# Whole score blocks, two-DMA clears and later head rows in a fused retention and mixture-of-experts kernel

## The chip, the cores and the metric

The kernel runs on one core of a Trainium2 chip. The metric is the device time of one execution in microseconds; the time of a kernel is the median of its runs.

## The reference

```python
# retention: B=4, H=8 heads, S=768, D=64, per-head decay gamma
for t in range(S):
    state = gamma * state + outer(k[:, :, t], v[:, :, t])
    y[:, :, t] = scale * (q[:, :, t] @ state)
x = y.transpose(0, 2, 1, 3).reshape(3072, 512)
# experts: E=8, D=512, F=1024; each token goes to one expert
logits = x @ w_gate
e_idx  = argmax(logits)
gate_w = softmax(logits)[e_idx]
eom    = sigmoid(x @ w_output_gate)
for e in range(8):
    mask = e_idx == e
    out[mask] = gate_w[mask] * eom[mask, e] * (relu(x[mask] @ w1[e]) @ w2[e])
```

## The kernel before

**Retention loop.** The 768 positions of a sequence are cut into six chunks of 128; four sequences give 24 steps (`NCH`), in two interleaved chains of sequences (`chunk`). In each step `n` TensorE multiplies the carried state with the queries (`inter`), forms the scores of the chunk (`scores`), turns the next chunk's keys (`kt_block`), multiplies the masked scores with the scaled values (`values`) and adds to the state (`state`). VectorE masks the scores (`masked`) and scales the outputs (`outputs`); GpSimd (POOL) multiplies the values with decays (`prep_v`); ScalarE (ACT) evicts. The scores of a head pair are 128 keys by 128 queries. Keys are loaded in two halves, and for heads 4 to 7 the halves of the partitions are exchanged (`load_keys`, three DMAs a load). The scores are computed per half of the keys: one matmul over all 128 queries, one over the 64 queries that the causal mask leaves for the late half (`x == 1`).

**Routing.** Two steps make a group. Its gate logits are formed, turned, and each token gets an expert (`route1`), a place in that expert's region (`counts`, `route2`) and a gate (`exps`, `gates`). The finished row is scaled (`rows_out`) and sent by GpSimd to its place in a sorted buffer in DRAM, `srt` (`scatter`), some four steps behind. A stretch of each region (rows `FILL` to `TOP`) is cleared beforehand with zeros from `zrow` (`clear`); clears and scatters write the same tensor, so a scatter waits for the clears that stand before it in program order, and a clear for the scatters before it.

**Head.** At step 14 (`PICK_AT`) the expert with the most tokens so far is picked (`totals`, `rank`); its weights are loaded one block of the hidden dimension at a time (`load_weights`, three DMAs into a ring `raw`) and split into a high and a low part (`split_high` on ACT, `split_low` on VectorE and GpSimd). At step 20 its first 256 rows are read back (`head_load`) and turned on VectorE (`head_prep`). Behind the loop, the expert's matmuls on these rows (`run_head(n)` issues n of them) are written between the last groups' routing and the ranking of all experts; `counts` and `totals` of the last group come there too.

**Experts.** The eight experts follow in ranked order (`mm1`, `mm2`, `relu1`), the first with 192 rows, the others with up to 448. Weights are loaded ahead as far as the ring allows.

The order on every engine is the order of the program, written by hand (`manual_schedule`); loads are issued by SyncE (SP) in order, `load_k(n + 3)` and `load_v(n + 3)` at the head of step `n`. Rings: keys 6, values 4, scaled values 3, raw weights 3.

## Time and profile before

| | us |
|---|---|
| median of 3 runs (480.23 to 483.4) | 480.68 |
| the profiled execution's own time | 483.37 |
| its span, first to last instruction | 481.4 |
| TensorE busy | 425.5 (88%) |
| VectorE busy | 227.5 (47%) |
| ScalarE busy | 190.3 (40%) |
| GpSimd busy | 254.1 (53%) |
| SyncE's queue of loads, share of 16 DMA engines | 53.5% |

The span is one execution on the chip. Busy times overlap between engines; a matmul's end is modelled, so a busy TensorE need not be at its peak.

### The profile page before, as it was taken

How to read it: one execution, taken by the hardware profiler on the slowest of the kernel's cores; microseconds unless marked ns; L12 is line 12 of the kernel's file. 1: busy time of each engine (PE TensorE's matmuls, PEld its weight loads, DVE VectorE, ACT ScalarE, POOL GpSimd, SP SyncE). 2: the span in 40 equal slices, each digit the busy share in tenths (PEclk: the TensorE clock that was granted, in tenths of full speed). 3: DMA queues.
4: the chain of work that ended last, by engine and by line, in shares of the span. 5: the costliest groups of instructions: out<-in, count | busy, mean ns of one | idle time of the engine just before them, and what ended most of it. 6: DMA issues, size and time to landing. Idle time of an engine off the chain costs nothing.

```text
span 481.4 us, 11599 instructions
## 1 busy us (share of the span) xinstructions
PE 425.5 (88%) x4080; PEld 393.9 (82%) x4080; DVE 227.5 (47%) x586; ACT 190.3 (40%) x375; POOL 254.1 (53%) x290
## 2 busy tenths in 40 slices
PE   7799359989895877979999999999999999999892
PEld 3578348768784777969999999999999999999771
DVE  3255045657664664427545445445445356354020
ACT  2346116545664231136434344345344444353010
POOL 3430165443661760363642667667676775885602
PEclk9799779999999689979999999999999999999987
DMA  6798788889874423835874864855855956850101
GB/s 149 161 203 205 196 217 212 192 206 224 206 199 119 131 107 91 169 92 155 204 168 121 178 174 142 188 173 155 197 149 154 222 164 174 206 164 21 46 1 67
DMA packets 130594, 75.85 MB, mean 158 GB/s; under 512 B 59444, under 2 KB 118200, under 8 KB 130496
## 3 DMA queue, kind: packets, MB, share of 16 engines
q1 hardware_dynamic: 124624, 61.54, 53.5%
q0 software_dynamic: 5136, 12.64, 7.7%
q8 instruction: 65, 1.06, 1.0%
q10 hardware_dynamic: 736, 0.34, 0.3%
q14 instruction: 33, 0.27, 0.2%
HBM read 59.73 MB, written 15.30 MB: 156 GB/s over the span
## 4 chain that ended last, share of the span: by engine, by line
PE 65%; DMA 7%; issue 7%; SPq 7%; DVE 6%; POOL 3%; ACT 2%; another core or an unknown queue 2%; POOLq 0%; DVEq 0%; ACTq 0%
PE h L859 24%; PE a L882 23%; PE y L380 4%; DMA kn<-in_k_dram 3%; SPq L243 3%; PE s L587 2%; PE y L345 2%; PE y L569 2%; POOL out_dram L200 1%; SPq L241 1%; PE px L491 1%; DMA vn<-in_v_dram 1%; DMA srt<-zrow 1%; PE s L359 1%
## 5 line engine op out<-in xcount | busy, mean ns | idle before, releaser
L193 POOL TENSOR_TENSOR wlo<-raw,whi 128x512 fp32r<-128x512 f32 x64 | 84.9, 1328 | 67.7 <-ACT whi L185 58.9
L200 POOL DMA_INDIRECT out_dram<-ot,idi x85 | 85.0, 1000 | 20.2 <-issue 18.5
L859 PE MATMUL h<-xw,whi 128*128 128x192 f32 (+7 forms) x256 | 86.0, 336 | 0.9 <-issue 0.7
L859 PE MATMUL h<-xh,whi 128*128 128x192 f32 (+7 forms) x256 | 85.9, 336 | 0.9 <-PE s L587 0.9
L859 PE MATMUL h<-xh,wlo 128*128 128x192 f32 (+7 forms) x256 | 85.4, 334 | 0.0
L869 DVE SCALAR_TENSOR_TENSOR hl<-h,hh 128x192 fp32r<-128x192 f32 (+7 forms) x64 | 35.4, 554 | 96.9 <-ACT hh L868 81.8
L882 PE MATMUL a<-hh,whi 128*128 128x192 f32 (+6 forms) x224 | 75.1, 335 | 2.8 <-ACT hh L868 2.8
L882 PE MATMUL a<-hl,whi 128*128 128x192 f32 (+6 forms) x224 | 75.0, 335 | 0.0
L882 PE MATMUL a<-hh,wlo 128*128 128x192 f32 (+6 forms) x224 | 74.8, 334 | 0.0
L868 ACT ACTIVATE hh<-h 128x192 fp32r<-128x192 f32 (+7 forms) x64 | 31.1, 488 | 88.7 <-PE h L859 66.7
L507 POOL DMA_INDIRECT srt<-row,pos x24 | 25.0, 1041 | 68.8 <-DMA srt<-zrow 15.3
L192 DVE TENSOR_TENSOR wlo<-raw,whi 128x512 fp32r<-128x512 f32 x61 | 42.9, 704 | 31.5 <-ACT whi L184 15.0
L184 ACT CAST whi<-raw 128x512 fp32r<-128x512 f32 x64 | 39.5, 618 | 45.4 <-PE a L882 25.8
L859 PEld LDWEIGHTS h<-xh,whi 128*128 128x128 f32 x256 | 49.1, 192 | 1.9 <-PE s L587 1.1
L859 PEld LDWEIGHTS h<-xw,whi 128*128 128x128 f32 x256 | 49.0, 192 | 1.9 <-issue 0.8
L859 PEld LDWEIGHTS h<-xh,wlo 128*128 128x128 f32 x256 | 49.1, 192 | 0.2
L370 DVE TENSOR_TENSOR am<-s,mask 128x512 f32<-128x512 f32 x48 | 30.9, 684 | 35.0 <-PE s L362 32.7
L882 PEld LDWEIGHTS a<-hh,whi 128*128 128x128 f32 x224 | 42.9, 191 | 3.4 <-ACT hh L868 3.0
L882 PEld LDWEIGHTS a<-hh,wlo 128*128 128x128 f32 x224 | 42.8, 191 | 0.3
L882 PEld LDWEIGHTS a<-hl,whi 128*128 128x128 f32 x224 | 42.7, 191 | 0.4
L380 PE MATMUL y<-am,vs 128*64 128x128 f32 x384 | 30.4, 305 | 13.8 <-DVE am L370 6.8
L185 ACT CAST whi<-raw 128x512 fp32r<-128x512 f32 x64 | 39.5, 617 | 0.4 <-DMA raw<-in_moe_w_dram 0.3
(160 smaller groups left out, 674.0 us busy)
## 6 DMA issues: line engine op xcount, KB each, us to landing
raw<-in_moe_w_dram SPq DMA_DIRECT2D x128, 128.0 KB
raw<-in_moe_w_dram SPq DMA_DIRECT2D x64, 256.0 KB
qn<-in_q_dram SPq DMA_DIRECT2D x12, 512.0 KB
kn<-in_k_dram SPq DMA_DIRECT2D x24, 128.0 KB
kn<-in_k_dram SPq DMA_DIRECT2D x48, 64.0 KB
vn<-in_v_dram SPq DMA_DIRECT2D x24, 128.0 KB
vn<-in_v_dram SPq DMA_DIRECT2D x48, 64.0 KB
xl<-srt SPq DMA_DIRECT2D x12, 209.6 KB
```

The lines of the kernel that those rows point to most:

```text
L184: nc.scalar.copy(hi[:, 0], raw[:, 0])
L185: nc.scalar.copy(perm(hi), r2)
L192: (first or nc.vector).tensor_sub(lo[:, 0], raw[:, 0], hi[:, 0].bitcast(F32))
L193: nc.gpsimd.tensor_sub(perm(lo), r2, perm(hi).bitcast(F32))
L200: st = nc.gpsimd.indirect_dma_start(out=dst, out_offset=bass.IndirectOffsetOnAxis(ap=idx, axis=0), in_=src, in_offset=None, bounds_check=n ...
L370: nc.vector.tensor_tensor(out=a.rearrange("p s o t -> p s (o t)"), in0=sp[b].rearrange("p (s x) -> p s x", s=2), in1=mask.rearrange("p o t ...
L380: nc.tensor.matmul(py(o, b, S_), vs[n][:, 2 * g + b], a[b][:, S_, o], start=(c == 0 and S_ == 0), stop=True, skip_group_check=True)
L507: s_ = nc.gpsimd.indirect_dma_start(out=srt, out_offset=bass.IndirectOffsetOnAxis(ap=rt.pop(("pos", i)), axis=0), in_=row.rearrange("p a x ...
L859: nc.tensor.matmul(ps[:, 0:C], l[:, 0, w], r[:, dc, 0:C], start=(n == 0), stop=(n == 3 * NDC - 1))
L868: nc.scalar.activation(hh, ps[:, 0:C], AF.Relu)
L869: nc.vector.scalar_tensor_tensor(out=hl, in0=ps[:, 0:C], scalar=0.0, in1=hh.bitcast(F32), op0=ALU.max, op1=ALU.subtract)
L882: nc.tensor.matmul(accs[d][:, 0:C], l[:, 1, w], r[:, 0:C], start=(f == 0 and n == 0), stop=(f == NF - 1 and n == 2))
```

## The change

- Keys and values are loaded whole, one DMA for each load, without the exchange of halves; the first values go through ACT's DMA queue, as does the clearing. The value decays are loaded straight into place.
- The scores of a head are one block of 128 keys by 128 queries: eight matmuls a step with 64 rows of contraction and 128 columns of weights, in place of sixteen. The mask is one 128 by 128 block.
- The clears are two DMAs of four regions each, at the end of steps 1 and 2, on ACT's queue, in place of eight at the head of steps 2 to 5 on SP's.
- At steps 14 and 18 the totals and the first operation that reads them come ahead of the scores.
- The weight blocks 0 to 5 are loaded at steps 17, 18, 19, 21, 22 and 23 (before: 0 to 7 at steps 15 to 22), 6 and 7 behind the loop and split after the ranking. The head's rows are turned at the ends of steps 22 and 23 (before: 21, and step 23 ahead of the logits).
- The last counts and totals are formed in the bank of the state, and 18 of the head's matmuls come ahead of the counts instead of 14.
- Rings: raw weights 4 (before 3), keys 5 (6), scaled values 2 (3). The exponential's table is loaded behind ACT's first DMA issues.

```diff
--- before.py
+++ after.py
@@ -84,12 +84,11 @@
     nc.vector.memset(wz, 0.0)
     warm = cpool.tile([P, 1], F32, name="warm")
     nc.vector.memset(warm, 0.0)
-    nc.scalar.activation(warm, warm, AF.Exp)
     ident = cpool.tile([P, P], F32, name="ident")
     make_identity(nc, ident)
 
     zrow = cpool.tile([P, ROW], F32, name="zrow")
-    mask = cpool.tile([P, 2, P], F32, name="mask")
+    mask = cpool.tile([P, P], F32, name="mask")
     ones_b = cpool.tile([P, P], BF16, name="ones_b")
     tri_b = cpool.tile([P, P], BF16, name="tri_b")
     io8i = cpool.tile([P, E], I32, name="io8i")
...
@@ -163,7 +160,7 @@
     def load_weights(s: int):
         r, f = divmod(s, NF)
         e = rank_e[r]
-        raw = wpool.tile([P, 8 * SEG], F32, name="raw", tag="raw", bufs=3)[:, 0:2 * DM].rearrange("p (w x) -> p w x", w=2)
+        raw = wpool.tile([P, 8 * SEG], F32, name="raw", tag="raw", bufs=4)[:, 0:2 * DM].rearrange("p (w x) -> p w x", w=2)
         for o in range(2):
             nc.sync.dma_start(
                 raw[o * HP:o * HP + HP, 0, :].rearrange("p (dc f) -> p dc f", f=P),
@@ -235,22 +232,15 @@
         kn, vn, qn, qr = {}, {}, {}, {}
         qt, kt, vs, yts, ams = {}, {}, {}, {}, {}
 
-        def load_keys(dst, src):
-
-            s = src.rearrange("h p d -> p h d")
-            nc.sync.dma_start(dst[:, 0:NG], s[:, 0:NG])
-            for x in range(2):
-                nc.sync.dma_start(dst[rows(x), NG:H], s[rows(1 - x), NG:H])
-
         def load_k(i):
             ch, b, c = chunk(i)
-            kn[i] = ap.tile([P, H, D], F32, name="kn", tag="kn", bufs=6)
-            load_keys(kn[i], k[b, :, c * P:(c + 1) * P, :])
-
-        def load_v(i):
+            kn[i] = ap.tile([P, H, D], F32, name="kn", tag="kn", bufs=5)
+            nc.sync.dma_start(kn[i], k[b, :, c * P:(c + 1) * P, :].rearrange("h p d -> p h d"))
+
+        def load_v(i, eng=nc.sync):
             ch, b, c = chunk(i)
             vn[i] = ap.tile([P, H, D], F32, name="vn", tag="vn", bufs=4)
-            load_keys(vn[i], v[b, :, c * P:(c + 1) * P, :])
+            eng.dma_start(vn[i], v[b, :, c * P:(c + 1) * P, :].rearrange("h p d -> p h d"))
 
         def load_q(ch, j):
             b, c = ch + 2 * (j // (NC // 2)), 2 * (j % (NC // 2))
@@ -280,30 +270,28 @@
             nc.vector.memset(sp[b], 0.0)
         load_q(0, 0)
         load_k(0)
-        load_v(0)
-        gva = ac.tile([P, 2, NC, H], F32, name="gva")
-        nc.scalar.dma_start(gva[:, 0], dec_v)
-        for x in range(2):
-            nc.scalar.dma_start(gva[rows(x), 1], dec_v[rows(1 - x)])
+        nc.scalar.dma_start(gv, dec_v)
+        load_v(0, nc.scalar)
         for o in range(2):
             nc.scalar.dma_start(gn[rows(o)].rearrange("p (b s) t -> p b (s t)", b=2),
                                 dec_q[:, 2 * o * P:2 * o * P + 2 * P].unsqueeze(0).broadcast_to([HP, 2, 2 * P]))
         nc.scalar.dma_start(ga.rearrange("p b c g -> p (b c g)"),
                             dec_c.rearrange("b x -> (b x)").unsqueeze(0).broadcast_to([P, 2 * NC * NG]))
+        nc.scalar.activation(warm, warm, AF.Exp)
         load_k(1)
         load_q(1, 0)
         load_v(1)
+        load_k(2)
         for o in range(2):
             for x, w in ((0, w_gate), (E, w_ogate)):
                 nc.sync.dma_start(wg[rows(o), :, x:x + E],
                                   w[o * DM // 2:(o + 1) * DM // 2].rearrange("(g p) e -> p g e", p=HP))
-        load_k(2)
         load_v(2)
         load_q(0, 1)
 
         def prep_v(i):
             ch, b, c = chunk(i)
-            vs[i] = ap.tile([P, H, D], F32, name="vs", tag="vs", bufs=3)
+            vs[i] = ap.tile([P, H, D], F32, name="vs", tag="vs", bufs=2)
             nc.gpsimd.tensor_mul(vs[i], vn.pop(i), gv[:, c, :].unsqueeze(2).broadcast_to([P, H, D]))
 
         def kt_block(i):
@@ -346,21 +334,12 @@
                                  start=(S_ == 0), stop=True, skip_group_check=True)
 
         def scores(n):
-            ch, ci = n % 2, n // 2
-            late = qt[ch, ci // 2].rearrange("p g r (c x j) -> p g r c x j", c=2, x=2)
             for S_ in range(2):
-                for x in range(2):
-
-                    for o in range(2):
-                        for b in range(2):
-                            g, y = 2 * o + S_, x ^ o
-                            w = sp[b][rows(y), (2 * S_ + o) * P:(2 * S_ + o) * P + P].rearrange("p (r z j) -> p r z j", r=2, z=2)
-                            if x == 0:
-                                nc.tensor.matmul(sp[b][rows(y), (2 * S_ + o) * P:(2 * S_ + o) * P + P], kt[n][rows(b), g, y * HP:y * HP + HP],
-                                                 queries(n, g, b), start=True, stop=True, skip_group_check=True)
-                            else:
-                                nc.tensor.matmul(w[:, :, 1], kt[n][rows(b), g, y * HP:y * HP + HP],
-                                                 late[rows(b), g, :, ci % 2, 1], start=True, stop=True, skip_group_check=True)
+                for o in range(2):
+                    for b in range(2):
+                        g = 2 * o + S_
+                        nc.tensor.matmul(sp[b][:, (2 * S_ + o) * P:(2 * S_ + o) * P + P], kt[n][rows(b), g], queries(n, g, b),
+                                         start=True, stop=True, skip_group_check=True)
 
         def masked(n):
             kt.pop(n)
@@ -368,8 +347,8 @@
             for b in range(2):
                 a = ap.tile([P, 2, 2, P], F32, name=f"am{b}", tag=f"am{b}", bufs=2)
                 nc.vector.tensor_tensor(
-                    out=a.rearrange("p s o t -> p s (o t)"), in0=sp[b].rearrange("p (s x) -> p s x", s=2),
-                    in1=mask.rearrange("p o t -> p (o t)").unsqueeze(1).broadcast_to([P, 2, 2 * P]), op=ALU.mult)
+                    out=a.rearrange("p s o t -> p (s o) t"), in0=sp[b].rearrange("p (x t) -> p x t", t=P),
+                    in1=mask.unsqueeze(1).broadcast_to([P, 4, P]), op=ALU.mult)
                 ams[n].append(a)
 
         def values(n):
@@ -448,10 +427,11 @@
             nc.scalar.activation(ex, rt.pop("d9"), AF.Exp)
             rt["ex"] = ex
 
-        def counts(grp):
+        def counts(grp, last=False):
             n = len(grp)
             oh = rt["oh"]
-            cnt = misc[:, 2 * P:2 * P + n * E]
+            cnt = st[:, 0, 0:n * E] if last else misc[:, 2 * P:2 * P + n * E]
+            rt["cnt"] = cnt
             nc.tensor.matmul(cnt, tri_b, oh.rearrange("p a e -> p (a e)"), start=True, stop=False, skip_group_check=True)
             for t in (cb, acc[:, 0], acc[:, 1]):
                 nc.tensor.matmul(cnt.rearrange("p (a e) -> p a e", e=E), ones_b, t.unsqueeze(1).broadcast_to([P, n, E]),
@@ -464,7 +444,7 @@
             oh = rt.pop("oh")
             nc.vector.tensor_tensor(out=acc[:, 0:n], in0=acc[:, 0:n], in1=oh, op=ALU.add)
             rk = small[:, 8 * E:10 * E].rearrange("p (a e) -> p a e", a=2)
-            nc.vector.tensor_tensor(out=rk, in0=misc[:, 2 * P:2 * P + n * E].rearrange("p (a e) -> p a e", e=E), in1=oh, op=ALU.mult)
+            nc.vector.tensor_tensor(out=rk, in0=rt.pop("cnt").rearrange("p (a e) -> p a e", e=E), in1=oh, op=ALU.mult)
             pos = sm.tile([P, 2], I32, name="pos", tag="pos", bufs=4)[:, 0:n]
             with nc.allow_low_precision("row numbers are whole"):
                 nc.vector.tensor_reduce(out=pos, in_=rk, axis=AX.X, op=ALU.add)
@@ -516,18 +496,23 @@
                         mybir.DependencyClass.Sync, mybir.DependencyReason.DATA), reason="sorted rows complete")
             sent.append(s_.ins)
 
-        def clear(e):
-            nc.sync.dma_start(srt[e * REG + FILL:e * REG + TOP, :], zrow[0:TOP - FILL])
-
-        def totals(upto):
-            tot = misc[:, 3 * P:3 * P + E]
+        def clear(e, n):
+            nc.scalar.dma_start(
+                srt[e * REG:(e + n) * REG].rearrange("(e r) x -> r e x", e=n)[FILL:TOP],
+                zrow[0:TOP - FILL].unsqueeze(1).broadcast_to([TOP - FILL, n, ROW]))
+
+        def totals(n):
+            tot = (misc[:, 3 * P:3 * P + E] if n < NCH else st[:, 0, 2 * E:3 * E])
             for a in range(2):
                 nc.tensor.matmul(tot, ones_b, acc[:, a], start=(a == 0), stop=(a == 1), skip_group_check=True)
             return tot
 
-        def rank(c8, last, by):
+        def rank_key(c8, last):
             key = sm.tile([P, E], F32, name="kk", tag="kk")
             nc.vector.scalar_tensor_tensor(out=key, in0=c8, scalar=float(E), in1=last, op0=ALU.mult, op1=ALU.add)
+            return key
+
+        def rank(key, by):
             top = sm.tile([P, E], F32, name="top", tag="top")
             nc.vector.max(out=top, in_=key)
             nc.vector.max_index(out=by, in_max=top, in_values=key)
@@ -537,7 +522,7 @@
         hd = {}
 
         def head_load():
-            t = wpool.tile([P, 8 * SEG], F32, name="xl0", tag="raw", bufs=3).rearrange("p (n x) -> p n x", x=SEG)
+            t = wpool.tile([P, 8 * SEG], F32, name="xl0", tag="raw", bufs=4).rearrange("p (n x) -> p n x", x=SEG)
             for a in range(4):
                 nc.sync.dma_start(
                     t[32 * a:32 * a + 32],
@@ -616,12 +601,10 @@
         PICK_AT = 14
         EARLY_AT = 18
         LOAD_AT = 20
-        w_at = {15 + j: j for j in range(NF)}
-        clear_at = {2: (0, 1), 3: (2, 3), 4: (4, 5), 5: (6, 7)}
+        w_at = {17: 0, 18: 1, 19: 2, 21: 3, 22: 4, 23: 5}
+        clear_at = {1: 0, 2: E // 2}
 
         constants_first()
-        for o in range(2):
-            nc.gpsimd.tensor_copy(gv[:, :, NG * o:NG * o + NG], gva[:, o, :, NG * o:NG * o + NG])
         prep_v(0)
         spread_gc()
         more_gq(0)
@@ -651,15 +634,23 @@
                 load_v(n + 3)
             for (ch, j) in q_load.get(n, ()):
                 load_q(ch, j)
-            for e in clear_at.get(n, ()):
-                clear(e)
             if n == PICK_AT + 1:
                 rank_e[0] = nc.values_load(pick[0:1, 0:1], engines=(ET.SP,), min_val=0, max_val=E - 1)
             if n in w_at:
                 load_weights(w_at[n])
             inter(n)
+            if n == PICK_AT:
+                by = rank_key(totals(n), io8)
+            if n == EARLY_AT:
+                cj = sm.tile([P, E], F32, name="cj", tag="cj")
+                nc.vector.scalar_tensor_tensor(out=cj, in0=totals(n), scalar=1.0, in1=first, op0=ALU.mult, op1=ALU.mult,
+                                               accum_out=cnt0)
             scores(n)
             masked(n)
+            if n == PICK_AT:
+                rank(by, pick)
+            if n == EARLY_AT:
+                nc.vector.tensor_scalar(out=late, in0=cnt0, scalar1=float(HEAD), scalar2=None, op0=ALU.is_lt)
             if n + 1 < NCH:
                 prep_v(n + 1)
             if even and n >= 4:
@@ -669,14 +660,6 @@
             if not even and n // 2 + 1 < NC:
                 more_gq(n // 2 + 1)
 
-            seen = totals(n) if n in (PICK_AT, EARLY_AT) else None
-            if n == PICK_AT:
-                rank(seen, io8, pick)
-            if n == EARLY_AT:
-                cj = sm.tile([P, E], F32, name="cj", tag="cj")
-                nc.vector.scalar_tensor_tensor(out=cj, in0=seen, scalar=1.0, in1=first, op0=ALU.mult, op1=ALU.mult,
-                                               accum_out=cnt0)
-                nc.vector.tensor_scalar(out=late, in0=cnt0, scalar1=float(HEAD), scalar2=None, op0=ALU.is_lt)
             if grp:
                 if even:
                     turn_logits(grp)
@@ -704,16 +687,17 @@
             if not even:
                 if grp:
                     gates(grp)
-                if n == NCH - 1:
-                    head_prep(1)
                 logits(group(n // 2), [0, 1])
                 keep_logits(group(n // 2))
             if not even and grp:
                 rows_out(n - 3)
+            if n == NCH - 1:
+                head_prep(1)
             if n == 0:
+                nc.gpsimd.memset(zrow, 0.0)
                 constants_second()
-            if n == 1:
-                nc.gpsimd.memset(zrow, 0.0)
+            if n in clear_at:
+                clear(clear_at[n], E // 2)
             if n == 2:
                 constants_third()
             if n == 6:
@@ -723,19 +707,21 @@
                 exps(grp)
             if n - 1 in w_at:
                 split_high(w_at[n - 1])
-            if n - 2 in w_at and n < 22:
-                split_low(w_at[n - 2], None if n in (17, 19) else nc.gpsimd)
+            if n - 2 in w_at:
+                split_low(w_at[n - 2], None if even else nc.gpsimd)
             if n == PICK_AT:
                 r0 = sm.tile([P, 1], F32, name="r0", tag="r0")
                 nc.vector.tensor_copy(r0, pick[:, 0:1])
                 nc.vector.tensor_scalar(out=first, in0=io8, scalar1=r0, scalar2=None, op0=ALU.is_equal)
             if n == LOAD_AT:
                 head_load()
-            if n == LOAD_AT + 1:
+            if n == LOAD_AT + 2:
                 head_prep(0)
 
 
         grp = group(NCH // 2 - 1)
+        for f in (NF - 2, NF - 1):
+            load_weights(f)
         scatter(NCH - 4)
         turn_logits(grp)
         tokens(NCH - 3)
@@ -743,18 +729,18 @@
         route1(grp)
         exps(grp)
         scatter(NCH - 3)
-        run_head(14)
-        counts(grp)
+        split_low(NF - 4)
+        split_high(NF - 3)
+        run_head(18)
+        counts(grp, True)
         route2(grp)
         gates(grp)
-        split_low(5)
+        split_low(NF - 3)
         run_head(12)
         for i in grp:
             tokens(i)
             rows_out(i)
             scatter(i)
-        split_low(6)
-        split_low(7)
         run_head(12)
         cnts = totals(NCH)
         cj = sm.tile([P, E], F32, name="cj", tag="cj")
@@ -762,7 +748,7 @@
                                        accum_out=cnth)
         io_ = sm.tile([P, E], F32, name="io_", tag="io_")
         nc.vector.scalar_tensor_tensor(out=io_, in0=first, scalar=-float(16 * NT), in1=io8, op0=ALU.mult, op1=ALU.add)
-        top = rank(cnts, io_, order)
+        top = rank(rank_key(cnts, io_), order)
         ordf = sm.tile([P, E], F32, name="ordf", tag="ordf")
         nc.vector.tensor_copy(ordf, order)
         nc.vector.tensor_sub(ck, top, ordf)
@@ -781,6 +767,8 @@
         on = sm.tile([P, 1], F32, name="on", tag="on")
         nc.vector.tensor_reduce(out=on, in_=dk, axis=AX.X, op=ALU.add)
         nc.vector.tensor_tensor(out=n_odd, in0=on, in1=late, op=ALU.add)
+        for f in (NF - 2, NF - 1):
+            split_weights(f)
 
     with ExitStack() as mctx:
         mp = mctx.enter_context(tc.tile_pool(name="mp", bufs=2))
```

## Rows read from the trace of the kernel before

**Rows 1.** Windows by stage: stretch, length, busy time of each engine, clock, DMA share, GB/s.

```profile
...
44.48:70.90 26.42, 13.46 (x214) 11.43 (x211) 6.70 (x23) 5.84 (x12) 9.42 (x26) 0.74 0.83 215
70.90:101.16 30.26, 28.28 (x565) 23.94 (x561) 19.84 (x70) 16.70 (x34) 17.16 (x23) 1.00 0.84 204
...
146.40:163.33 16.93, 11.31 (x180) 9.39 (x177) 7.36 (x26) 5.22 (x11) 8.09 (x9) 0.76 0.45 126
163.33:199.24 35.91, 29.22 (x234) 27.80 (x234) 21.22 (x72) 9.41 (x22) 10.54 (x12) 0.92 0.47 123
199.24:228.46 29.22, 25.50 (x190) 24.59 (x191) 13.09 (x30) 11.65 (x26) 15.79 (x14) 0.88 0.43 121
228.46:446.89 218.43, 218.43 (x1221) 215.88 (x1222) 106.66 (x199) 93.00 (x174) 145.50 (x129) 1.00 0.64 164
...
```

**Rows 2.** Timeline of TensorE: start, length, operation, [idle before, what ended it].

```profile
...
56.78 1.97 PE L380 MATMUL y<-am,vs 128*64 128x128 f32 x16 [6.09 <-POOL vs L307]
...
155.55 1.98 PE L380 MATMUL y<-am,vs 128*64 128x128 f32 x16 [4.78 <-DVE am L370]
...
```

**Rows 3.** Timeline of GpSimd, steps 4 to 6.

```profile
...
54.32 1.20 POOL L507 DMA_INDIRECT srt<-row,pos  x1 [15.34 <-DMA srt<-zrow]
...
55.68 1.05 POOL L307 TENSOR_TENSOR vs<-vn,gv 128x512 f32<-128x512 f32 x1
...
```

**Rows 4.** Timeline of SyncE's queue: issue of DMAs, steps 0 to 5.

```profile
...
22.84 1.30 SPq L243 DMA_DIRECT2D vn<-in_v_dram  x2
...
47.09 1.95 SPq L520 DMA_DIRECT2D srt<-zrow  x2
...
```

**Rows 5.** Windows of 2 us with their DMA share and GB/s.

```profile
...
12.00:14.00 2.00, 1.42 (x32) 1.28 (x31) 0.79 (x2) 0.56 (x1) 0.56 (x1) 1.00 1.24 313
...
28.00:30.00 2.00, 2.00 (x60) 1.76 (x60) 1.77 (x9) 0.96 (x2) 1.85 (x10) 1.00 1.14 201
...
44.00:46.00 2.00, 2.00 (x36) 1.76 (x38) 1.49 (x7) 0.80 (x2) 0.00 (x0) 1.00 1.12 371
...
```

**Rows 6.** Timeline of VectorE, the first queries.

```profile
...
5.24 0.76 DVE L318 COPY qr<-qn 128x512 f32<-128x512 f32 x2 [2.74 <-DMA qn<-in_q_dram]
...
```

**Rows 7.** Timeline of TensorE, step 14, the turned logits.

```profile
...
105.96 0.44 PE L420 MATMUL misc<-ident,lt 128*128 128x128 f32 x2 [1.34 <-DVE kk L530]
...
```

**Rows 8.** Timeline of TensorE and its weight load, steps 12 and 13; group of a line.

```profile
...
93.19 0.45 PE L359 MATMUL s<-qt,kt 64*64 64x128 f32 x8
...
94.02 0.44 PE L420 MATMUL misc<-ident,lt 128*128 128x128 f32 x2
...
95.26 1.09 PE L380 MATMUL y<-am,vs 128*64 128x128 f32 x16
96.18 0.64 PE L389 MATMUL st<-vs,kn 128*64 128x64 f32 x16
...
98.83 0.17 PE L455 MATMUL misc<-oh,tri_b 128*128 128x16 bf16 x1 [0.60 <-ACT ex L448]
...
95.26 0.85 PEld L380 LDWEIGHTS y<-am,vs 128*64 128x64 f32 x16 [0.17 <-issue]
...
L359 PE MATMUL s<-qt,kt 64*64 64x128 f32 x384 | 20.2, 288 | 0.7 <-ACT qt L328 0.7
...
```

**Rows 9.** Timelines of VectorE and of SyncE's queue, steps 20 to 22.

```profile
...
154.05 0.77 DVE L554 STREAM_TRANSPOSE xt<-xl 128x256 f32<-128x256 f32 x2 [6.49 <-DMA xl<-srt]
...
147.73 1.93 SPq L542 DMA_DIRECT2D xl<-srt  x4
...
```

**Rows 10.** Timelines of TensorE and VectorE in the tail behind the loop.

```profile
...
171.16 0.17 PE L455 MATMUL misc<-oh,tri_b 128*128 128x16 bf16 x1 [2.49 <-ACT ex L448]
...
174.94 1.28 DVE L192 TENSOR_TENSOR wlo<-raw,whi 128x512 fp32r<-128x512 f32 x2
...
177.90 3.27 DVE L767 CAST ordf<-order 128x8 f32<-128x8 uint32 x1
...
```

**Rows 11.** Timeline of GpSimd in the first expert pass.

```profile
...
209.43 1.28 POOL L193 TENSOR_TENSOR wlo<-raw,whi 128x512 fp32r<-128x512 f32 x1
...
```

8 lines of the change are left out of this document (3 added, 5 removed).

## Prediction

> **What bounds the kernel now.** I read the stages first: windows whose edges are the ends of a step's last value matmuls [rows 1]. From 228.46 to 446.89 TensorE is busy 218.43 of 218.43 us: the experts' matmuls, untouched by the diff. So the 33 us behind them and this stretch stay, and what the change is worth lies before 228.46. There the steps differ. Six steps from 70.90 to 101.16 take 30.26 us, 5.04 each, with TensorE busy 28.28: that is what a step costs when nothing is late. Steps 6 and 7 take 26.42 us for two, steps 22 and 23 take 16.93, and the clock granted to TensorE there is 0.74 and 0.76. The tail behind the loop takes 35.91 us, the first pass of the experts 29.22 with 25.50 busy.
>
> Second view: who TensorE waits for in the slow steps. Step 6's values wait 6.09 us for POOL's scaled values, step 22's 4.78 us for the masked scores [rows 2]. POOL's own row says why in step 6: its first scatter waits 15.34 us for a clear of the sorted rows [rows 3], and the scaled values of the next step are queued behind it. The clears come late because they stand in SP's queue behind key and value loads: six issues of some 0.65 us for a step's keys and values, and the clears of step 4 issued from 47.09 on [rows 4]. The clears of step 5 come in program order behind that first scatter and must wait for it, the second scatter for them: so the two queues block each other twice, and step 7 is slow too.
>
> **The early loads (steps 0 to 5).** A step's keys and values go from six issues to two, the first values to ACT's queue, the clears (8 x 258 KB, 2.11 MB) into steps 1 and 2 on ACT's queue. Then the data, not SP, sets these steps. To step 5's values it must bring 12 blocks of 262 KB (3.15 MB), 5 query blocks (2.62 MB), 0.3 MB of decays and the clears. Near-pure stretches show the rates [rows 5]: 201 GB/s for 256-byte keys and values, 313 where queries prevail, 371 where clears do. That is 15.7 + 8.4 + 1.5 + 5.7 = 31.3 us. The first query block, 1.7 us of it, is in at 5.24 [rows 6], so step 5's values land near 34.8; scaling (1.05) and the value matmuls (1.1) follow, and I add 2.5 for imperfect overlap: step 5 ends near 39.5 instead of 44.48. Gain 5.0. Ends: what is left behind the first block (7.7 MB) all at 201 GB/s gives 5.24 + 38.1 + 2.2 = 45.5, a loss of 1; without my 2.5 the gain is 7.5.
>
> The DMA page of the Trainium skill ("DMA: Bandwidth & Descriptors", Rules for kernel authors) says that spreading DMAs over SP, ACT and GpSimd gives no bandwidth, since all run on the same 16 engines. By it alone the move to ACT wins nothing here and the clears only push 5.7 us of loads back; the trace agrees that bytes are the limit (DMA share 1.14 at 201 GB/s). What the move changes is order, and that is the next part.
>
> **The clears and the scatters (steps 6 and 7).** The clears no longer stand behind loads, and are issued two steps before the first scatter. By step lengths (an estimate) ACT reaches them near 20 and 25, 2.85 us of data each at 371 GB/s, some 6 when shared; the first scatter is due after step 5's values were scaled, near 36. So POOL's 15.34 vanishes, and step 7's wait behind it. What is late next in these steps is TensorE itself: 2 x 5.04 = 10.1 for 26.42, **gain 16.3**. If a clear still held the scatter for 5 us, TensorE would lose about 3, since its need comes a step later.
>
> **Steps 14 and 18.** The totals' matmuls and their first VectorE operation move ahead of the scores; today TensorE's next transposes wait 1.34 us for it [rows 7], and in step 18 as long again. The scores, 0.83 us, now cover it. Gain 2.7; if uncovered, 0.
>
> **Score blocks.** Before: 32 instructions, 0.83 us from the first to the next operation (93.19 to 94.02) [rows 8]. After: 16 of 64x128, 128 columns wide. No row shows that form. Nearest: the values, 16 instructions on half the array, 128 columns: 0.92 us (95.26 to 96.18). That is +0.09, plus a change of array form between the carried-state matmuls (64x64) and the scores, which today have the same form; where the form changes into the values', the weight load's row shows 0.17 us idle. So +0.26 a step. Ends: the smaller instruction count wins the switch back, 0; or two blocks don't overlap, twice the values' 0.92, +1.18 with the switch. In odd steps TensorE waits anyway, 0.60 us for ACT's exponentials [rows 8], which hides 0.26. So 12 x 0.26, plus a little in odd steps: **loss 3.5**, ends 0 and 28.
>
> The Trainium skill's "TensorEngine Tiling (Array Packing)" (Key Properties) says that changing the tiling mode drains TensorE. The 0.17 idle agrees in sign. Without such a drain the term would be 12 x 0.09 = 1 and the time 2.5 us lower.
>
> **Weights and head rows (steps 15 to 23).** SP issues nine DMAs a step there now; with loads whole and weights two steps later it has five or fewer, and head rows are asked for right after their scatter, not at 147.73 behind a weight load. Today VectorE, in order, waits 6.49 us for them at 154.05 with step 22's mask behind it [rows 9]; turning them a step later adds 5 us of cover. Steps 22 and 23 fall from 16.93 to 10.1 + 0.3: gain 6.5. Next late is POOL: its scatter of step 21 still waits for that read, with split work (2.5 us) and step 23's values behind it: I take 1 off, ends 0 and 3. The value ring of 2 and the key ring of 5 cost nothing as long as POOL scales values a step ahead of need, as it does by the 5 us between its rows; if POOL is late, they cost what it is late.
>
> **Tail.** Counts go to the state's bank, so TensorE no longer waits for ACT's exponentials behind a weight split: 2.49 us [rows 10]. Against it, the VectorE halves of the last two splits (0.64 us each) now stand between the routing chain and the head's next hidden block; that chain has a cast of eight numbers in it that takes 3.27 us, and TensorE waits for the block behind it today. Two more weights are split in the tail, but run_head needs them 15 us later. Net **gain 1.5**, from -3 (the last weight lands late, behind the head rows' buffer) to +5 (the cast takes 0.2 as its neighbours do).
>
> **First expert pass.** A fourth raw buffer lets one more weight block load while the head runs; today POOL's subtraction, which frees the third, comes only at 209.43, behind the head's scatters [rows 11]. TensorE is idle 3.7 us in this pass; how much of it hangs on loads no row says, so I take 1, ends 0 and 5 (its granted clock of 0.88 could rise too).
>
> Everything else (mask of one block, table load behind ACT's issues, no copies of the value decays) is in the first 9 us beside loads: 0.
>
> **How the numbers follow.** 5.0 + 16.3 + 2.7 + 6.5 - 1 - 3.5 + 1.5 + 1 = 28.5. The profiled execution took 483.37 (span 481.4), as long as the longest of the three runs, whose median is 480.68. 483.37 - 28.5 = 454.9; from the median **452**, which I forecast. Chance 0.68, with 445 to 460 as its own width.
>
> **Rivals.** (1) Order is not enough: the interleaved clears and whole blocks leave the early steps bound by bytes, no gain there and half of steps 6 and 7 lost to late loads: 452 + 5 + 8 = 465. For it: a DMA share of 0.83 and 0.84 in the loop [rows 1]. Against: loads run four steps ahead once SP is free. 0.14. (The DMA page's rule above would lead here.) (2) Score blocks don't overlap: 24 x 1.18 - 3.5 = 24.8 more, 477. Against: the values overlap in halves. 0.08. (3) The tail eats more: the last weight's DMA waits for the head rows' buffer and VectorE stands still behind it, with TensorE: 5 to 8 us, 458. 0.05. (4) Slower than before: score blocks that run one at a time and unpipelined, each from its start to its end (288 ns is the mean of one in [rows 8]; 16 of them 4.6, +3.8 a step): 452 + 91 - 3.5 = 540. It decides from 1.3 us a step (28.5 + 3.5 over 24). Against: no split form in the trace does so. 0.05.
>
> A measurement of this kernel tells some 1% (4.8 us) from no change. Faster by over 1%: forecast, (1), (3) and half of (2), 0.91; within 1% half of (2), 0.04; slower 0.05. The range goes from 444 to 467: rival (1) and the widths of score blocks and tail are in it, (2) and (4) out.
>
> **What would show it.** In the changed profile: POOL's first scatter waits under 3 us for a clear and TensorE's row before step 6's values shows no wait for POOL; step 5 ends near 39.5, step 23 near 137; the scores take 1.0 to 1.1 from start to next; no wait of 1.3 before the turned logits in steps 14 and 18; VectorE's head transposes without a wait of 6 us; the experts' steady stretch still 218 us. The forecast is wrong if the steps of 5.04 themselves grow (score blocks, or loads now in the chain), or if the stalls only move to the tail, where weights 6 and 7 load last.

## The result and the profile after

The changed kernel takes 465.19 us (median of 4 runs, 464.45 to 466.21) against 481.05 for the kernel before: a ratio of 0.9664, 95% interval 0.9624 to 0.9705. That is 15.9 us faster where 28.5 was forecast; the time lies inside the range of 444 to 467, near its upper end, and outside the width of 445 to 460 that the forecast gave itself. The profiled execution has a span of 464.2 us, 17.2 below that of before. One execution of all (676.85 us at a granted clock of 0.557, in the first run of 5) was in the chip's slow state and is left out of every ratio.

The changed kernel by windows: the nine stages are steps 0 to 5, 6 and 7, 8 to 13, 14 to 21, 22 and 23, the tail, the first expert pass (first matmul to the second expert's first), the other passes up to the last expert, and the rest. Columns as in [rows 1].

```profile
0.00:45.14 45.14, 38.22 (x474) 29.40 (x476) 19.29 (x57) 18.37 (x36) 18.91 (x44) 0.96 1.02 231
45.14:55.93 10.79, 10.63 (x182) 8.91 (x179) 6.52 (x23) 5.86 (x12) 6.76 (x22) 1.00 0.95 240
55.93:87.17 31.24, 29.80 (x468) 24.89 (x465) 19.74 (x70) 16.82 (x34) 14.60 (x19) 1.00 0.98 235
87.17:132.29 45.12, 42.44 (x706) 35.64 (x704) 28.80 (x103) 24.72 (x51) 20.65 (x25) 1.00 0.68 174
132.29:142.94 10.65, 9.27 (x148) 7.22 (x145) 7.23 (x25) 4.27 (x9) 6.71 (x8) 1.00 0.68 199
142.94:182.15 39.21, 29.75 (x234) 28.33 (x234) 24.54 (x73) 11.76 (x27) 15.92 (x17) 0.87 0.54 138
182.15:209.42 27.27, 23.82 (x180) 23.40 (x181) 11.85 (x28) 10.37 (x23) 14.99 (x14) 0.87 0.40 113
209.42:417.50 208.08, 206.99 (x1155) 204.42 (x1154) 103.54 (x192) 90.35 (x169) 137.74 (x122) 1.00 0.67 170
417.50:464.17 46.67, 36.76 (x181) 31.45 (x180) 9.07 (x19) 7.44 (x15) 17.80 (x18) 0.92 0.11 34
```

Against [rows 1] (steps 0 to 5 ended at 44.48, steps 14 to 21 lasted from 101.16 to 146.40), with the forecast in brackets: steps 0 to 5 +0.7 (-5.0); steps 6 and 7 -15.6 (-16.3); steps 8 to 21 +0.9 (-2.7 for steps 14 and 18, some +2 for the score blocks); steps 22 and 23 -6.3 (-5.5); the tail +3.3 (-1.5). For the first pass, cut in the same way, the kernel before has one more row:

```profile
199.24:226.07 26.83, 23.31 (x181) 22.88 (x181) 11.38 (x26) 10.23 (x23) 14.49 (x14) 0.87 0.40 112
```

So +0.4 there (-1), and -0.6 behind it, where nothing was changed. Two terms carry most of the 11.3 us between the two sums of the spans (28.5 and 17.2): 5.7 in the early steps and 4.8 in the tail.

**Steps 6 and 7.** Timeline of GpSimd: the first scatters go out with no wait for a clear, where one of 15.34 stood [rows 3].

```profile
39.13 1.20 POOL L487 DMA_INDIRECT srt<-row,pos  x1 [0.17 <-ACT row L478]
41.71 1.03 POOL L487 DMA_INDIRECT srt<-row,pos  x1 [0.17 <-POOL vs L295]
```

**Step 14.** Timeline of TensorE: the turned logits start without a wait, where one of 1.34 stood [rows 7].

```profile
90.99 0.44 PE L399 MATMUL misc<-ident,lt 128*128 128x128 f32 x2
```

**Early steps.** Timelines of SyncE's queue, ACT's queue and TensorE: the keys of step 4 are issued at 20.08, in the same moment as the first clear of 1 MB. Step 3 has to turn these keys and waits 2.21 us for them.

```profile
20.08 1.03 SPq L238 DMA_DIRECT2D kn<-in_k_dram  x1
...
20.17 0.41 ACTq L500 DMA_DIRECT2D srt<-zrow  x1
...
28.93 0.63 PE L300 MATMUL pk<-ident,kn 128*128 128x128 f32 x4 [2.21 <-DMA kn<-in_k_dram]
```

The window behind that wait, with TensorE at half clock (0.50, the lower of its two levels):

```profile
30.00:32.00 2.00, 2.00 (x29) 1.88 (x26) 1.27 (x5) 0.24 (x2) 0.84 (x1) 0.50 1.09 292
```

Step 2 had ended at 23.77, 4.3 us ahead of before (28.07); step 3 takes 7.27 for 4.79, and by step 5 the lead is gone.

**Tail.** Timelines of VectorE, GpSimd and TensorE, and the window behind the wait. Two operations of the ranking on eight numbers take 3.1 us each (the second row is two operations, 3.30 in all), and each ends where a pair of GpSimd's subtractions ends: 153.30 + 3.11 = 156.41 beside 153.84 + 2.54 = 156.38, and 158.51 + 3.30 = 161.81 beside 159.29 + 2.48 = 161.77. Behind the ranking come the splits, and behind them the hidden block for which TensorE waits 5.71 us. It then runs at half clock for 5.52.

```profile
153.30 3.11 DVE L750 SCALAR_TENSOR_TENSOR io__2522<-first,io 128x8 f32<-128x8 f32 x1
158.51 3.30 DVE L763 SCALAR_TENSOR_TENSOR up<-dk,up 128x8 f32<-128x8 f32 x2
...
153.84 2.54 POOL L190 TENSOR_TENSOR wlo<-raw,whi 128x512 fp32r<-128x512 f32 x2
159.29 2.48 POOL L190 TENSOR_TENSOR wlo<-raw,whi 128x512 fp32r<-128x512 f32 x2
...
164.18 0.58 PE L572 MATMUL s<-h,whi 128*128 128x256 f32 x1 [5.71 <-DVE h L560]
...
164.18:169.70 5.52, 5.52 (x26) 5.52 (x27) 0.28 (x1) 0.21 (x1) 0.00 (x0) 0.50 0.16 41
```

### The profile page after: what moved, and what is told of

The parts are those of the page before. It is cut to its first block, busy times and chain, and to the rows that moved or that the text cites. A ratio compares the mean times of both kernels' runs of the same rounds, so it can differ in the third digit from the quotient of the medians.

```text
span 464.2 us, 10645 instructions
## 1 busy us (share of the span) xinstructions
PE 427.7 (92%) x3696; PEld 393.6 (85%) x3696; DVE 230.6 (50%) x586; ACT 190.0 (41%) x375; POOL 254.1 (55%) x286
## 3 DMA queue, kind: packets, MB, share of 16 engines
q8 instruction: 62, 1.02, 0.9%
## 4 chain that ended last, share of the span: by engine, by line
PE 76%; issue 6%; DVE 5%; POOL 5%; DMA 4%; another core or an unknown queue 2%; ACT 1%; SPq 1%; POOLq 0%; DVEq 0%; ACTq 0%
PE h L847 27%; PE a L870 25%; PE y L359 4%; PE s L341 4%; PE pq L314 3%; PE s L572 3%; PE y L554 2%; DMA kn<-in_k_dram 2%; PE px L471 2%; PE y L333 2%; PE st L368 1%; POOL out_dram L197 1%; PE pk L300 1%; PE misc L388 1%
## 5 line engine op out<-in xcount | busy, mean ns | idle before, releaser
L856 ACT ACTIVATE hh<-h 128x192 fp32r<-128x192 f32 (+7 forms) x64 | 31.2, 489 | 90.9 <-PE h L847 76.0
L295 POOL TENSOR_TENSOR vs<-vn,gv 128x512 f32<-128x512 f32 x24 | 25.0, 1044 | 43.9 <-PE st L368 17.2
```

Of the source, the lines that this page charges most:

```text
L295: nc.gpsimd.tensor_mul(vs[i], vn.pop(i), gv[:, c, :].unsqueeze(2).broadcast_to([P, H, D]))
L856: nc.scalar.activation(hh, ps[:, 0:C], AF.Relu)
```

## Experiments

The runs fell on chips that differ. The kernel before took 480.9 to 481.5 in three groups and 474.0 to 474.6 in two; on the latter, the second kind below, the first expert pass is 22.5 us instead of 26.1 to 27.5, in every version. The loop differs too: steps 6 to 23 of the same program took 97.80 and 97.91 us on the first kind (the changed kernel and its second run) and 95.35 on the second (the second version of 8). So a ratio is always to the kernel before in the same group. Runs 1, 3, 4 and 5 were on the second kind, where neither the kernel before nor the changed kernel alone was profiled: a difference of that size between their stages and those of the first kind may be the chip's.

**1. The clears alone, on the kernel before.**

```diff
-        clear_at = {2: (0, 1), 3: (2, 3), 4: (4, 5), 5: (6, 7)}
+        clear_at = {1: 0, 2: E // 2}
...
-            for e in clear_at.get(n, ()):
-                clear(e)
...
+            if n in clear_at:
+                clear(clear_at[n], E // 2)
...
```

> The kernel before, with the clears alone changed: two DMAs of four regions at the ends of steps 1 and 2 on ACT's queue. My theory: the clears behind the loads in SP's queue made steps 6 and 7 slow, so these two fall from 26.42 us to 11 or 12 and the time falls by 13 to 16 us, to 465 to 468; the early steps may lose 1 to 2 of it. Rival A: the loads themselves (six issues of 0.65 us for a step's keys and values) are what is late, and with eight clears fewer on SP's queue only 5 us go: 476. Rival B: clears in steps 1 and 2 push loads back by their 5.7 us and give back a third of the gain: 471.

Measured: ratio 0.9968 (0.9929 to 1.0006), 472.93 for 474.02. All three forecasts fail: they gave gains of 13 to 16, 5 and 10 us, and 1.1 came. Its windows of steps 6 and 7, 14 to 21, 22 and 23, then SyncE's queue and VectorE:

```profile
48.25:59.55 11.30, 10.02 (x213) 8.56 (x211) 6.51 (x23) 5.97 (x12) 6.42 (x23) 1.00 0.92 212
...
89.35:137.67 48.32, 40.82 (x834) 35.18 (x832) 29.18 (x103) 25.45 (x52) 24.92 (x30) 0.96 0.84 213
137.67:160.13 22.46, 13.09 (x180) 10.71 (x177) 7.32 (x25) 7.00 (x14) 9.14 (x10) 0.67 0.51 135
...
107.46 1.45 SPq L168 DMA_DIRECT2D raw<-in_moe_w_dram  x2
...
142.10 1.43 SPq L168 DMA_DIRECT2D raw<-in_moe_w_dram  x2
...
145.19 1.93 SPq L544 DMA_DIRECT2D xl<-srt  x4
...
150.86 0.77 DVE L556 STREAM_TRANSPOSE xt<-xl 128x256 f32<-128x256 f32 x2 [12.03 <-DMA xl<-srt]
```

Steps 6 and 7 win their 15.1 us, as forecast. Then most of it is given back: 3.8 in the early steps, 3.1 in steps 14 to 21, 5.5 in steps 22 and 23. Five step lengths lie between the weight blocks issued at 107.46 and at 142.10, 6.9 us each: SP with its nine issues a step is slower than TensorE's 5.04. The head's rows are asked for at 145.19, 2.5 us earlier than in [rows 9], though the loop ran 11 us ahead at step 7; VectorE waits 12.03 us for them in place of 6.49. In the kernel before, SP's queue was a second bound behind the first.

**2. Whole loads alone, on the kernel before** (scores in halves over the straight keys; clears, weights, head rows and tail as before).

```diff
-            nc.sync.dma_start(dst[:, 0:NG], s[:, 0:NG])
-            for x in range(2):
-                nc.sync.dma_start(dst[rows(x), NG:H], s[rows(1 - x), NG:H])
+            nc.sync.dma_start(dst, s)
...
```

> The kernel before, with keys and values loaded whole and the scores in halves over the straight keys; clears, weights, head rows and tail as before. The clears alone won 1.5 us, since SP's queue (nine issues, 7 us a step from step 15 on) then set when the head's rows were asked for. If that queue is the common bound, whole loads alone shorten steps 22 and 23 by 4 to 6 and let the clears out earlier: steps 6 and 7 at 20 to 24 for 26.42, in all 8 to 14 us. If the clears' place decides by itself, steps 6 and 7 stay as they are and only the 6 us of steps 22 and 23 go, less than 7 in all.

Measured: ratio 0.974 (0.967 to 0.981), 470.03 for 481.5. Windows of steps 0 to 5, 6 and 7, 22 and 23:

```profile
0.00:39.50 39.50, 34.06 (x570) 25.77 (x572) 19.05 (x57) 18.31 (x36) 15.02 (x41) 1.00 1.05 216
39.50:63.11 23.61, 14.15 (x213) 12.09 (x211) 6.87 (x23) 5.84 (x12) 10.15 (x27) 0.78 1.05 230
...
139.62:149.95 10.33, 8.73 (x180) 6.99 (x177) 7.51 (x26) 4.25 (x9) 6.88 (x7) 1.00 0.34 92
```

The first forecast holds (8 to 14 us in all, steps 6 and 7 at 20 to 24), and the common bound is shown: with two issues a step for keys and values in place of six, steps 22 and 23 fall by 6.6, although head rows and weights stand where they stood. It wasn't the bytes, which are the same: the first three weight blocks are issued 4.4 us apart here (100.47, 104.89 and 109.19), where they lay 6.8 apart in the kernel before (five steps from 110.95 to 144.91). Steps 6 and 7 keep most of their wait. Step 5 ends at 39.50, the very number forecast for the changed kernel, but that is chance: the forecast's sum had the clears' 5.7 us ahead of step 5's values, and here SP issues all clears behind them.

```profile
25.37 1.14 SPq L241 DMA_DIRECT2D vn<-in_v_dram  x1
26.61 2.08 SPq L517 DMA_DIRECT2D srt<-zrow  x2
```

**3. The old clears in the changed kernel** (eight DMAs on SP, steps 2 to 5).

```diff
-        clear_at = {1: 0, 2: E // 2}
+        clear_at = {2: (0, 1), 3: (2, 3), 4: (4, 5), 5: (6, 7)}
...
+            for e in clear_at.get(n, ()):
+                clear(e)
...
-            if n in clear_at:
-                clear(clear_at[n], E // 2)
...
```

> The changed kernel with the clears as before: eight DMAs on SP's queue at the heads of steps 2 to 5. If the place in the program decides (clears of steps 4 and 5 stand behind loads and behind the first scatters), GpSimd's scatter waits again and the time goes up by 10 to 15 us, to 475 to 480. If SP's long queue of loads was the cause, whole loads have cured it already (two issues a step) and the time rises by less than 4, to 465 to 469, perhaps falls because the clears no longer compete with steps 2 to 4.

Measured: ratio 0.9698 (0.9665 to 0.973). Windows of steps 0 to 5 and 6 and 7, and the matmuls that turn the keys of step 4:

```profile
0.00:41.22 41.22, 35.25 (x475) 26.43 (x476) 19.15 (x57) 18.45 (x36) 14.27 (x38) 1.00 1.03 216
41.22:62.37 21.15, 12.47 (x181) 10.30 (x179) 6.48 (x23) 5.85 (x12) 9.89 (x26) 0.84 0.96 233
...
26.83 0.63 PE L300 MATMUL pk<-ident,kn 128*128 128x128 f32 x4
```

Neither forecast alone: the old place of the clears costs 10.4 us in steps 6 and 7 (10.79 in the changed kernel) and wins 3.9 by step 5 (45.14). TensorE doesn't wait for the keys of step 4 here; in all nine profiles of versions with the early clears once and whole loads it does, from 1.71 to 6.31 us (2.21 in the changed kernel), and step 5 ends between 42.91 and 47.90. So the early clears delay the loads, and how much varies from profile to profile. Whether by their bytes alone or by the place they take in the order isn't settled, as the next run shows.

**4. Each clear written twice** (once into a spare tensor that nothing reads).

```diff
-            nc.scalar.dma_start(
-                srt[e * REG:(e + n) * REG].rearrange("(e r) x -> r e x", e=n)[FILL:TOP],
...
+            for t in (spare, srt):
+                nc.scalar.dma_start(
+                    t[e * REG:(e + n) * REG].rearrange("(e r) x -> r e x", e=n)[FILL:TOP],
...
```

> The changed kernel, each clear written a second time into a spare tensor that nothing reads (2.06 MB more on ACT's queue in steps 1 and 2). If steps 3 to 5 are bound by bytes, as I hold now (they lost the 4.3 us that step 2 was ahead), the end of step 5 moves from 45.1 to 50 or 51 and the time rises by 4 to 6 us, to 470. If what is late there is SP's issue, or TensorE's work, the end of step 5 moves by less than 1.5 and the time by less than 2.

Measured: ratio 0.9676 (0.9647 to 0.9705), step 5 ends at 49.63. The forecast of bytes (50 or 51) is nearly met at step 5, but not by its mechanism. Whether the time rose by the 4 to 6 us forecast can't be told: the changed kernel's 0.9664 and 0.9607 come from the other kind of chip. ACT's queue and TensorE:

```profile
31.83 0.41 ACTq L502 DMA_DIRECT2D spare<-zrow  x1
...
33.70 0.17 PE L436 MATMUL misc<-oh,tri_b 128*128 128x16 bf16 x1 [6.95 <-ACT ex L428]
```

The clears of step 2, issued at 24.86 in the changed kernel, go out at 31.83 here; ACT's exponentials stand behind them in ACT's order, and TensorE behind those. So a DMA that went out late on ACT's queue held ACT's own work; what held the DMA, the trace doesn't say. The run doesn't price the bytes.

**5. Scores in halves again, over keys loaded whole** (two runs).

```diff
-                        nc.tensor.matmul(sp[b][:, (2 * S_ + o) * P:(2 * S_ + o) * P + P], kt[n][rows(b), g], queries(n, g, b),
...
+                            g, y = 2 * o + S_, z ^ o
+                            s = sp[b][rows(y), (2 * S_ + o) * P:(2 * S_ + o) * P + P]
+                            w = kt[n][rows(b), g, y * HP:y * HP + HP]
+                            if y == 0:
+                                nc.tensor.matmul(s, w, queries(n, g, b), start=True, stop=True, skip_group_check=True)
...
+                                                 late[rows(b), g, :, ci % 2, 1], start=True, stop=True, skip_group_check=True)
```

> The changed kernel with the scores in halves of the keys again (32 instructions, 64 columns of weights, half of them over 64 queries), over keys loaded whole. Traces: the blocks take 1.10 us where the halves took 0.83, and 0.17 us of idle weight load stands before them where the carried state's matmuls come first. If the form costs that, even steps fall from 6.02 to 5.6 and the time falls by 4 to 6 us, to 459 to 461. Rival: without the exchanged halves of the keys a quarter of the array with 64 queries waits for one with 128, so the halves take 0.95 to 1.0 and 1 to 3 us are won: 462 to 464. Or the steps are bound by other engines by now: no change.

> The changed kernel with the scores in halves, a second time, since its ratio of 0.947 came from another chip than the changed kernel's own 0.961 and 0.966. If the halves win by themselves, odd steps are 0.2 shorter than the changed kernel's and the ratio is 0.945 to 0.955 here too. If they win only where VectorE's masks aren't late, odd steps are longer here (5.3 for 5.1), even ones 0.24 shorter, and the ratio is 0.960 to 0.966.

Measured: 0.9471 (0.9432 to 0.9509) and 0.9539 (0.9481 to 0.9597). First the changed kernel (TensorE, then its weight load), then the halves:

```profile
79.51 1.16 PE L341 MATMUL s<-qt,kt 64*128 64x128 f32 x16
80.61 0.44 PE L399 MATMUL misc<-ident,lt 128*128 128x128 f32 x2
...
74.18 0.97 PEld L341 LDWEIGHTS s<-qt,kt 64*128 64x128 f32 x16 [0.17 <-issue]
```

```profile
78.20 0.33 PE L347 MATMUL s<-qt,kt 64*64 64x128 f32 x2
...
79.22 0.44 PE L407 MATMUL misc<-ident,lt 128*128 128x128 f32 x2
```

From first to next the blocks take 1.10 us (79.51 to 80.61), the halves 1.02, and the halves of the exchanged keys 0.83 [rows 8]; the 0.17 of the changed form comes on top for the blocks. Steps 8, 10 and 16 take 5.59 us each before, 6.02 with blocks (0.27 and 0.16 more), 5.78 with halves. Two runs of one group on the second kind of chip compare steps 6 to 23, blocks (the version of 8 below, whose loop is that of the changed kernel) and halves:

```profile
46.53:141.88 95.35, 92.00 (x1484) 76.64 (x1481) 61.40 (x219) 51.67 (x106) 48.66 (x74) 1.00 0.80 206
```

```profile
47.90:140.82 92.92, 88.58 (x1773) 74.59 (x1769) 61.99 (x219) 51.60 (x106) 48.60 (x74) 1.00 0.81 206
```

Halves win 2.4 us there: the size of the rival that gave 1 to 3, with odd steps 0.2 shorter (step 9 takes 4.54 for 4.77), as the second run's first forecast had it. On the first kind of chip they lost as much: in 8, steps 6 to 23 took 100.34 with halves against 97.91 for the unaltered kernel run again. Why odd steps differ between chips is open.

**6. The tail's two suspects.** (a) GpSimd's halves of splits 4 to 7 to VectorE; (b) 30 of the head's matmuls, with their hidden blocks, written into the ranking; beside them the changed kernel unaltered.

```diff
-        nc.gpsimd.tensor_sub(perm(lo), r2, perm(hi).bitcast(F32))
+        (second or nc.gpsimd).tensor_sub(perm(lo), r2, perm(hi).bitcast(F32))
...
+        run_head(6)
         io_ = sm.tile([P, E], F32, name="io_", tag="io_")
...
+        run_head(24)
         ordf = sm.tile([P, E], F32, name="ordf", tag="ordf")
```

> The changed kernel unaltered, on the chip of this group, as the base for the other three. The kernel before took 474.0 on the last chip and 481.1 on the first, with 4.4 us of the difference in each of the first and the last expert pass, which the change doesn't touch; so I expect the same difference of 15 to 18 us here, whatever the chip: a ratio of 0.963 to 0.968.

> The changed kernel with the halves that GpSimd subtracts in splits 4 to 7 given to VectorE (four more subtractions of 0.64 us on VectorE, none on GpSimd behind the loop but split 3). In the trace two ranking operations on eight numbers take 3.1 us each and end within 0.05 us of the end of a pair of GpSimd's subtractions. If VectorE waits there for GpSimd, both fall to 0.2, the ranking is 6 us shorter less 2.6 for the subtractions, and the time falls by 2 to 4 us. If the 3.1 us have a cause of their own (code, a queue), they stay, VectorE has 2.6 us more to do and the time rises by 2 to 3.

> The changed kernel with 30 of the head's matmuls, and the hidden blocks that VectorE makes of them, written into the ranking ahead of the two last splits (6 after the first ranking operation, 24 after the order is known). If TensorE's 6.9 us of waiting in the tail, and the 5.5 us at half clock behind it, come from VectorE's order (the hidden block stands behind the ranking and the splits), the tail falls from 39 to 31 to 34 us and the time by 5 to 8. Rival: the experts' first rows or weights, which hang on the ranking, are late next, and the wait only moves there: 0 to 3 us.

Measured: unaltered 463.71 us, 0.9607 (0.9533 to 0.968), tail 39.01; (a) 460.13, 0.9526 (0.9446 to 0.9606), tail 34.08; (b) 460.64, 0.9565 (0.9488 to 0.9642), tail 36.49. So (a) wins 3.6 us, as its first forecast said, and (b) 3.1, the size of its rival. VectorE and TensorE of (a):

```profile
153.52 0.16 DVE L750 SCALAR_TENSOR_TENSOR io__2522<-first,io 128x8 f32<-128x8 f32 x1
...
155.68 0.37 DVE L763 SCALAR_TENSOR_TENSOR up<-dk,up 128x8 f32<-128x8 f32 x2
...
159.63 0.39 PE L572 MATMUL s<-h,whi 128*128 128x256 f32 x1 [1.42 <-DVE h L560]
```

The same two operations take 0.16 and 0.37 when GpSimd has nothing to subtract: VectorE had waited for GpSimd. The cast of 3.27 us in the kernel before looks like the same: it ends at 181.17 [rows 10], and the one pair of GpSimd's subtractions there at 181.13; no run took that pair away.

```profile
178.59 2.54 POOL L193 TENSOR_TENSOR wlo<-raw,whi 128x512 fp32r<-128x512 f32 x2
```

In (b) they stay slow; the first hidden block comes earlier, and the next one waits again, for VectorE's ranking and splits and not for the experts' rows that the rival named:

```profile
156.59 3.42 DVE L765 SCALAR_TENSOR_TENSOR up<-dk,up 128x8 f32<-128x8 f32 x2
...
162.38 0.39 PE L572 MATMUL s<-h,whi 128*128 128x256 f32 x1 [3.80 <-DVE h L560]
```

The Trainium skill, "SBUF — State Buffer" (SBUF: two separate sides), says that VectorE and GpSimd share one pair of ports as an exclusive lock: a VectorE operation that takes both its port pairs, or that has two inputs in SBUF against a GpSimd operation that reads SBUF, can't run beside GpSimd's, and the one that starts first holds the lock for its whole instruction. These runs agree in the end of the wait, which is that of GpSimd's subtractions, and in its going when they go. The start they don't show: in the changed kernel VectorE's operation begins 0.54 us ahead of GpSimd's pair by the profile (153.30 and 153.84), and it waits for both instructions of the pair, not for one.

**7. Head rows turned where they were** (end of step 21; in step 23 ahead of the logits).

```diff
-            if n == LOAD_AT + 2: head_prep(0)
+            if n == LOAD_AT + 1: head_prep(0)
...
+                if n == NCH - 1: head_prep(1)
                 logits(group(n // 2), [0, 1])
```

> The changed kernel with the head's rows turned where they were before: at the end of step 21 and, in step 23, ahead of the logits. The trace of the changed kernel has their read issued from 128.68 to 130.64 (before: from 147.73) and landed by 134.2, where step 21 ends at 132.3. If the shorter queue of SP, which asks for them earlier, is what won the 6.3 us of steps 22 and 23, VectorE waits 2 us here and the two steps grow by 1 to 2. If the later place (5 us of cover, as I predicted) won them, they grow by 4 to 6 and the time with them.

Measured: ratio 0.9646 (0.9598 to 0.9694). Its window of steps 22 and 23 and VectorE's first turn of the head's rows, then SyncE's queue and GpSimd in the changed kernel:

```profile
133.62:143.75 10.13, 9.27 (x148) 7.23 (x145) 7.36 (x25) 4.24 (x9) 7.97 (x9) 1.00 0.69 206
...
134.79 0.77 DVE L539 STREAM_TRANSPOSE xt<-xl 128x256 f32<-128x256 f32 x2
```

```profile
128.68 1.96 SPq L527 DMA_DIRECT2D xl<-srt  x4
...
134.22 1.03 POOL L487 DMA_INDIRECT srt<-row,pos  x1 [5.03 <-DMA raw<-in_moe_w_dram]
```

The two steps don't grow (10.13 for 10.65), where even the small forecast had 1 to 2; VectorE turns the rows without a wait. The later place won nothing; the earlier request won all of the 6.3. Counted from the end of step 20, the rows are asked for 1.1 us later in the changed kernel, 0.9 here, 1.8 in 2, 5.6 in the kernel before and 11.8 in 1; VectorE waits for them 0, 0, 1.43, 6.49 and 12.03 us.

**8. Together.** (a) and (b) of 6 with the scores in halves, and without.

> The changed kernel with the scores in halves again, 30 of the head's matmuls written into the ranking, and GpSimd's halves of splits 4 to 7 given to VectorE. The parts on their own: the tail 4.9 us shorter by the splits; the head's matmuls 2.5 by themselves, of which some 1 is left beside it; the halves 0.24 in even steps and 0.2 to 0.3 in odd ones where TensorE doesn't wait, some 4. Together 8 to 10 us below the changed kernel's 463.7: 454 to 456, a ratio to the kernel before of 0.942 to 0.948. If the parts overlap more (the experts' first rows set the end of the tail), 458.

> The changed kernel (whole score blocks kept) with 30 of the head's matmuls written into the ranking and GpSimd's halves of splits 4 to 7 given to VectorE. The version with both and the scores in halves had the tail at 31.3 us but a loop 1.6 us longer than that of the split change alone. If the halves caused that, this one has the tail at 31 to 32 and the loop at 142 to 143: a ratio of 0.945 to 0.950. If the early loads' chance decides (step 5 has ended anywhere from 42.9 to 46.3 with the same loads), it stays at 0.952 to 0.957.

Measured: with halves 0.954 (0.9499 to 0.9581), 459.0; without 0.9399 (0.9354 to 0.9443), 446.62 for 474.56. The first misses its forecasts (454 to 456, at most 458), the second is better than either of its own. The tail is 31.3 and 31.2 us. The tail of the second run of 5, which has the changed kernel's tail and ran in the second version's group, then TensorE's last wait for VectorE in the second version's:

```profile
140.82:179.52 38.70, 29.35 (x234) 27.92 (x234) 24.51 (x73) 11.77 (x27) 15.89 (x17) 0.91 0.58 146
...
159.49 0.38 PE L572 MATMUL s<-h,whi 128*128 128x256 f32 x1 [0.29 <-DVE h L560]
```

The second version beats the kernel before by 6%, and its interval lies below both of the changed kernel's; but that one ran on the first kind of chip only. What stands against the same kind is the tail, 31.22 for 38.70: some 7.5 us.

## Why the prediction was right or wrong

**Right: the clears and the scatters** (16.3 forecast, 15.6 measured). GpSimd's wait went, and steps 6 and 7 fell to 10.79. But the term was written as if it stood alone, and 1 shows that it doesn't: without whole loads the same 15 us are won and most of them given back, 3.8 in the early steps and 8.6 behind SP's queue. The ends of step 7 and step 23 tell it: before 70.90 and 163.33; clears alone 59.55 and 160.13; whole loads alone 63.11 and 149.95; both 55.93 and 142.94.

**Right in size, for another reason: head rows** (6.5 less 1; measured 6.3). I named both causes, SP's shorter queue and 5 us of cover by the later turn. 7 shows that the first did it all; GpSimd's scatter did wait there, 5.03 us (the profile names a weight load, the read was in flight too), with nothing late behind it. The forecast of 5.5 counts the score blocks' 0.3 twice, here and in their own term.

**Wrong: the early loads** (-5.0; measured +0.7). The failing step is the sum of bytes with 2.5 us "for imperfect overlap". It put the clears into the sum as 5.7 us that any order could absorb. Whole loads with the clears behind them end step 5 at 39.50 and 41.22 (2 and 3); clears issued beside the keys of step 4 cost these 2.2 us of wait, with half clock behind it, and step 5 ends at 45.14. Whether bytes or order did it stays open. Rival (1) had this half right: no gain in the early steps, though not its loss in steps 6 and 7. That the measured 465 is rival (1)'s number is luck: its 8 us in steps 6 and 7 didn't come, and the tail's 4.8 took their place.

**Wrong: the tail** (-1.5; measured +3.3). The wait for ACT's exponentials went as forecast, and the mechanism against it was named: two splits between the ranking and the head's next hidden block, and a cast of 3.27. What failed is the size and the nature of that 3.27. It was taken for a cast's own oddity that might go; by 6 it is VectorE waiting for GpSimd, and the change put two pairs of subtractions beside the ranking in place of one. Without them, in 6 (a), the tail is 34.08, 1.8 below before: near the 1.5 of the forecast. Rival (3) has the place and the price (5 to 8; measured 4.8 off the forecast), not the cause.

**Mis-sized: score blocks** (+0.26 an even step; measured +0.43). The switch is as priced (0.16 for 0.17); the blocks took 1.10 us, not the 0.92 of the values that stood in for them. Their weight load took 0.97 for the values' 0.85 [rows 8]; that the 128 columns of weights in place of 64 are the reason is likely, but no run changes them alone. Steps 14 and 18 fell by 0.99 and 1.20 with that in them, so their own term is 3.05 where 2.7 was forecast. **Nothing:** the first pass; TensorE's 3.5 us of idle time there (23.31 busy of 26.83, now 23.82 of 27.27) stayed with a fourth raw buffer. (The prediction's "33 us" behind the experts' stretch are 34.5, from 446.89 to 481.4; no sum uses them.)

## What to carry to other kernels

A stall that is removed is worth what lies between it and the next queue that is full: count the issues per step of each DMA queue against the step's length (here 6.9 us against 5.04) before adding up gains, since here two parts were worth 1 and 11.5 us alone, and the whole change 16. A clear or any large write that is moved forward should be set against the load that is needed next, not against the mean rate of the stretch. Where a tiny VectorE operation takes microseconds, look which GpSimd instruction ends in the same moment; here moving that work took 4.9 us off the tail, and writing other work in front of it 2.5.

## What was not expected of the hardware

VectorE operations on eight numbers took 3.1 to 3.3 us beside GpSimd's subtractions and 0.16 without them. VectorE's record of such an operation starts before GpSimd's and counts the wait as busy. A 1 MB clear on ACT's queue went out 7 us late in one run (31.83 for 24.86), and ACT's next operation with it. One program was 1.5% apart on two kinds of chip (481 and 474); the first expert pass took 26.1 to 27.5 us on the one and 22.5 on the other, whatever the version.
